# A mixture of experts behind an attention: the first layer's matmul with weights stationary and tokens moving

## The chip, the cores and the metric

The kernel runs on one core of one Trainium2 chip. The metric is the device time of one execution in microseconds (us), less being better. TensorE is called PE in the profile's rows (PEld is its weight load), VectorE DVE, ScalarE ACT, GpSimd POOL and SyncE SP.

## The reference

Two stages, in float32.

- **Attention.** q, k and v are 8 batches x 8 heads x 576 positions x 64. A coarse attention over positions averaged by four, and a local one within a band of three positions on either side, are added. The result is seen as 4608 tokens of 512 values.
- **Experts.** Each token goes to the one of eight experts whose embedding it is most alike (cosine, divided by a temperature); `gate_w` is the softmax weight of that expert. For the tokens of expert e:

```
h = np.maximum(x[mask] @ w1[e], 0.0)
out[mask] = gate_w[mask, None] * (h @ w2[e])
```

w1[e] is 512 x 1024, w2[e] is 1024 x 512.

## The kernel before

**Attention phase** (from the start to about 320 us of the trace). It goes over 32 units (a batch and a pair of heads) in a software pipeline, writes each batch's tokens with their expert scores to a scratch `xd` in HBM, and keeps each token's expert and its rank. The first expert's weights are prepared beside it.

**Expert phase** (from about 320 to 803 us). The tokens, sorted by expert, fill slots of 128 (`SLOT`); 41 slots run here, and five more stand behind a branch that is not taken. Each slot q goes through these steps:

- `gather` (POOL): an indirect DMA brings the slot's 128 token rows into `xg`.
- `x_size` and `x_split`: the tokens are scaled by a power of two and split into two fp16 halves (high and low), one on ACT, the other on DVE. A transposing DMA on SP's queue (line 1030) makes `xT`, with the 512 values on the partitions in four pieces and the tokens along the free dimension.
- `mm1` (line 1066): for each half n of the 1024 hidden values, 12 matmuls in `mm1_half` (lines 1076 to 1078) fill one PSUM bank [128 tokens, 512]. The stationary operand is a 128x128 piece of `xT`, and 512 columns of w1 move. There are three products for each of the four pieces k: x high with w1 high, x high with w1 low, x low with w1 high.
- `hidden`: ACT writes relu as fp16 (line 1085), DVE the remainder as fp16 (line 1086), both into `h2` [tokens, 2, 512], of which there are two buffers. A transposing DMA on SP's queue (line 1089) makes half of `hT`, with the hidden values on the partitions. It is two such DMAs a slot.
- `mm2_part`: 24 matmuls (lines 1101 to 1103) with a 128x128 piece of `hT` stationary and 512 columns of w2 moving. `out_rows` scales by the gate on ACT, and `store` writes the rows with an indirect DMA on POOL's queue.

`run_slots` writes the order out by hand. For slot q it is mm1(q), with hidden(q); the test for new weights; the next gather; x_size and x_split of slot q+2; then mm2(q-1), its output and store. So PE runs mm1(q), mm2(q-1), mm1(q+1), mm2(q), and hT(q) has from the end of mm1(q) to the end of mm1(q+1) to arrive.

**A change of expert** happens seven times. The weights (float32, staged in `st`) are split into fp16 high and low by `split_all`, in four pieces of 128x1024: `w1h` on ACT (line 773), `w1l` on DVE (line 774). Piece p of w1 holds two of the four k (by p % 2) and half the hidden values (by p // 2), so pieces 0 and 1 make up half n = 0. The split of w1 stands between mm1(q) and mm1(q+1), that of w2 behind mm2(q-1). After the split, SP loads the next expert's 2 MB into `st` (line 866); that load stands in SP's queue ahead of the transpose for xT(q+2). Where the flag says that no new weights are needed, these loads move nothing.

SP's queue, in program order for a slot: two transposes for hT, the loads of w1, the transpose for xT(q+2), the loads of w2. POOL's queue carries gathers and stores.

**The way into the phase** (`run`, lines 1140 to 1193): mm1(0) is interleaved with the end of the attention by calls of `mm1_half` with a range of k; then come mm1(1), the first three pieces of mm2(0), the lists of the first four slots (`ids_of`, line 594: PE, then DVE), x_split(2), the rest of mm2(0), mm1(2).

Of the kernel before, what the change touches and what calls it, by code (L numbers as in the profile page):

```python
# [9 lines left out]
F16 = mybir.dt.float16  # L10
BF16 = mybir.dt.bfloat16
I32 = mybir.dt.int32
AF = mybir.ActivationFunctionType
ALU = mybir.AluOpType
# [6 lines left out]
N, DM, E, FF = B * S, H * D, 8, 1024  # L21
# [9 lines left out]
SLOT = 128  # L31
# [17 lines left out]
class Kern:  # L49
# [1017 lines left out]
        for n in range(2):  # L1067
            self.hidden(q, n, self.mm1_half(q, n))

    def mm1_half(self, q, n, k0=0, k1=DM // 128, ps=None):  # L1070

        nc, xT = self.nc, self.sl[q]["xT"]
        ps = self.bank() if ps is None else ps
        ns = slice(n * 512, (n + 1) * 512)
        for k in range(k0, k1):
            nc.tensor.matmul(out=ps, lhsT=xT[:, 0, k], rhs=self.w1h[:, k, ns], start=(k == 0), stop=False)  # L1076
            nc.tensor.matmul(out=ps, lhsT=xT[:, 0, k], rhs=self.w1l[:, k, ns], start=False, stop=False)  # L1077
            nc.tensor.matmul(out=ps, lhsT=xT[:, 1, k], rhs=self.w1h[:, k, ns], start=False, stop=(k == self.KC - 1))  # L1078
        return ps

    def hidden(self, q, n, ps):

        nc, s = self.nc, self.sl[q]
        h2 = self.hd.tile([SLOT, 2, 512], F16, name="h2")
        nc.scalar.activation(out=h2[:, 0], in_=ps, func=AF.Relu)  # L1085
        nc.vector.scalar_tensor_tensor(out=h2[:, 1], in0=ps, scalar=0.0, in1=h2[:, 0], op0=ALU.max, op1=ALU.subtract)  # L1086
        if not n:
            s["hT"] = self.hd.tile([128, 2, 2, 4, SLOT], F16, name="hT")
        nc.sync.dma_start_transpose(out=s["hT"][:, n].rearrange("p t c s -> p (t c) s"),
                                    in_=h2.rearrange("p a f -> p (a f)"))  # L1090

    def mm2(self, q):
        self.out_rows(q, self.mm2_part(q))
# [1 line left out]
    def mm2_part(self, q, j0=0, j1=FF // 128, ps=None):  # L1095

        nc, s = self.nc, self.sl[q]
        ps = self.bank() if ps is None else ps
        for j in range(j0, j1):
            hh, hl = (s["hT"][:, j // 4, t, j % 4] for t in range(2))  # L1100
            nc.tensor.matmul(out=ps, lhsT=hh, rhs=self.w2h[:, j, :], start=(j == 0), stop=False)  # L1101
            nc.tensor.matmul(out=ps, lhsT=hh, rhs=self.w2l[:, j, :], start=False, stop=False)  # L1102
            nc.tensor.matmul(out=ps, lhsT=hl, rhs=self.w2h[:, j, :], start=False,  # L1103
                             stop=(j == self.FC - 1))
        return ps
# [134 lines left out]
```

## Time and profile before

| | |
|---|---|
| median of three runs | 820.86 us (820.54 to 826.13) |
| the profiled execution | 818.35 us, of it a span of 816.6 us from the first instruction to the last |
| PE busy, share of the span | 725.5 us, 89% |
| PE weight loads | 424.7 us, 52% |
| DVE, ACT, POOL busy | 520.1, 514.4, 400.9 us |
| mean granted TensorE clock | 0.950 |
| queue q1 (SP), share of 16 DMA engines | 64.5% |

Times in rows are in us from the span's start unless marked ns. "Idle before" is time in which the engine did nothing ahead of an instruction, with what ended it. A granted clock of 1.00 is TensorE at 2.4 GHz, 0.50 at 1.2 GHz. A matmul's recorded duration is that of one through its pipeline; they overlap, so the pace of a row of them is read from start to start.

### The profile page before, as it was taken

The page shows a single profiled execution, that of the slowest core. Times are in us where ns is not written, and L with a number is a line of the kernel's source. Part 1 is how long each engine was busy: PE and PEld are TensorE (multiplying, and loading weights), DVE is VectorE, ACT ScalarE, POOL GpSimd, SP SyncE. Part 2 cuts the span into 40 slices and gives each one's busy share as a digit, 9 for nine tenths or more (in the row PEclk, how much of TensorE's full clock was granted, in tenths as well). Part 3 has the DMA queues.
Part 4 walks back from the last instruction along what each step waited for, and adds up shares of the span by engine and source line. Part 5 has one row for each costly group of instructions (what it writes and reads, how often), then busy time and mean ns, then how long its engine had stood idle before and what let it go on. Part 6 is the DMA issues. An engine that isn't in the chain of part 4 may idle for free. (4 is left out here: it accounts for less than half of the span.)

```text
span 816.6 us, 22314 instructions
## 1 busy us (share of the span) xinstructions
PE 725.5 (89%) x7588; PEld 424.7 (52%) x7588; DVE 520.1 (64%) x1597; ACT 514.4 (63%) x1159; POOL 400.9 (49%) x783
## 2 busy tenths in 40 slices
PE   7799799988899989688989899989998998999993
PEld 4577677766677766343444444434443444444441
DVE  7698798998789898574735647364653355456420
ACT  6678788889779764236754767566664356547520
POOL 6364645475454563364544455564554435544421
PEclk9899898999889889899999999999999999999997
DMA  7578787877767736946887978889698659759750
GB/s 177 122 185 204 196 200 147 222 141 230 121 180 149 183 65 205 214 117 114 224 167 127 282 151 233 181 218 226 173 213 136 133 159 215 162 111 256 146 104 18
DMA packets 246901, 138.93 MB, mean 170 GB/s; under 512 B 177106, under 2 KB 223186, under 8 KB 246752
## 3 DMA queue, kind: packets, MB, share of 16 engines
q1 hardware_dynamic: 238944, 116.05, 64.5%
q0 software_dynamic: 6560, 19.03, 8.8%
q10 hardware_dynamic: 1248, 2.11, 1.0%
q8 instruction: 62, 1.02, 0.6%
q14 instruction: 87, 0.71, 0.3%
HBM read 213.05 MB, written 20.33 MB: 286 GB/s over the span
## 5 line engine op out<-in xcount | busy, mean ns | idle before, releaser
L1076 PE MATMUL bank<-w1h,xT 128*128 128x512 f16 x328 | 126.0, 384 | 16.2 <-DMA xT<-x 10.3
L1101 PE MATMUL bank<-w2h,hT 128*128 128x512 f16 x328 | 125.8, 383 | 15.1 <-DMA hT<-h 15.1
L1077 PE MATMUL bank<-w1l,xT 128*128 128x512 f16 x328 | 125.6, 383 | 1.3 <-DVEq L921 1.3
L1078 PE MATMUL bank<-w1h,xT 128*128 128x512 f16 x328 | 125.6, 383 | 0.0
L1102 PE MATMUL bank<-w2l,hT 128*128 128x512 f16 x328 | 125.6, 383 | 0.0
L1103 PE MATMUL bank<-w2h,hT 128*128 128x512 f16 x328 | 125.6, 383 | 0.0
L347 ACT ACTIVATE kq<-bank 64x288 f32<-64x288 f32 x256 | 109.7, 429 | 20.9 <-PE bank L343 16.2
L1086 DVE SCALAR_TENSOR_TENSOR h<-bank,h 128x512 f16<-128x512 f32 x82 | 55.2, 690 | 99.2 <-ACT h L1085 76.3
L1085 ACT ACTIVATE h<-bank 128x512 f16<-128x512 f32 x82 | 47.8, 594 | 103.9 <-PE bank L1078 53.9
L1114 POOL DMA_INDIRECT out_dram<-o,ids x41 | 45.7, 1116 | 133.9 <-ACTq L916 101.4
L361 POOL TENSOR_TENSOR pool_kq<-kq 128x288 f32<-128x288 f32 x62 | 41.6, 677 | 87.8 <-ACT kq L347 86.1
L998 POOL DMA_INDIRECT xg<-xd,ids x41 | 45.8, 1117 | 51.0 <-POOLq L922 15.5
L749 ACT ACTIVATE junk<-st 128x1024 bf16<-128x1024 f32 (+1 forms) x30 | 67.6, 2254 | 4.2 <-issue 2.8
L1076 PEld LDWEIGHTS <-xT 128*128 128x128 f16 x328 | 32.3, 99 | 55.5 <-DMA xT<-x 17.3
L1101 PEld LDWEIGHTS <-hT 128*128 128x128 f16 x328 | 34.7, 106 | 50.9 <-DMA hT<-h 16.2
L370 POOL TENSOR_TENSOR pool_v<-ld_v 72x256 f32<-72x256 f32 x64 | 47.0, 750 | 23.4 <-DMA ld_v<-in_v_dram 23.2
L1046 ACT ACTIVATE lg<-lg,lmx 128x8 f32<-128x8 f32 x41 | 12.3, 301 | 73.1 <-DVE lmx L1044 73.1
L67 POOL TENSOR_SCALAR nw_t<-nw_y,nw_a 128x1 f32<-128x1 f32 x120 | 52.4, 437 | 12.1
L409 ACT ACTIVATE ad<-bank,md 72x144 f32<-72x144 f32 x128 | 46.5, 370 | 18.6 <-DVE md L403 15.5
L1028 DVE SCALAR_TENSOR_TENSOR x<-xg,sc,x 128x512 f16<-128x512 f32 x41 | 30.9, 753 | 40.3 <-ACT x L1025 40.2
L1077 PEld LDWEIGHTS <-xT 128*128 128x128 f16 x328 | 32.4, 99 | 41.7 <-issue 5.7
L1078 PEld LDWEIGHTS <-xT 128*128 128x128 f16 x328 | 32.4, 99 | 41.2 <-issue 3.3
(220 smaller groups left out, 1592.1 us busy)
## 6 DMA issues: line engine op xcount, KB each, us to landing
st<-in_moe_w_dram SPq DMA_DIRECT2D x148, 1024.0 KB
ld_k<-in_k_dram SPq DMA_DIRECT2D x64, 144.0 KB
ld_q<-in_q_dram SPq DMA_DIRECT2D x64, 144.0 KB
ld_v<-in_v_dram SPq DMA_DIRECT2D x32, 288.0 KB
vw<-in_v_dram SPq DMA_DIRECT2D x64, 144.0 KB
xd<-xr SPq DMA_DIRECT2D x8, 1040.0 KB
st<-in_moe_w_dram SPq DMA_DIRECT2D x12, 512.0 KB
st<-in_moe_w_dram ACTq DMA_DIRECT2D x4, 512.0 KB
```

The costliest lines, as they stand in the source:

```text
L67: g.tensor_scalar(out=t, in0=y, scalar1=y, scalar2=a, op0=ALU.mult, op1=ALU.mult)
L347: nc.scalar.activation(out=kq[h * D:(h + 1) * D, w, 3 + r:3 + r + S:2], in_=ps[r * D:(r + 1) * D], func=AF.Copy)
L370: g.tensor_tensor(out=t6[:, c], in0=vr[:, :, 0:2 * D], in1=vr[:, :, 2 * D:], op=ALU.add)
L749: self.nc.scalar.activation(out=junk, in_=src, func=AF.Square, accum_out=acc)
L1076: nc.tensor.matmul(out=ps, lhsT=xT[:, 0, k], rhs=self.w1h[:, k, ns], start=(k == 0), stop=False)
L1077: nc.tensor.matmul(out=ps, lhsT=xT[:, 0, k], rhs=self.w1l[:, k, ns], start=False, stop=False)
L1078: nc.tensor.matmul(out=ps, lhsT=xT[:, 1, k], rhs=self.w1h[:, k, ns], start=False, stop=(k == self.KC - 1))
L1085: nc.scalar.activation(out=h2[:, 0], in_=ps, func=AF.Relu)
L1086: nc.vector.scalar_tensor_tensor(out=h2[:, 1], in0=ps, scalar=0.0, in1=h2[:, 0], op0=ALU.max, op1=ALU.subtract)
L1101: nc.tensor.matmul(out=ps, lhsT=hh, rhs=self.w2h[:, j, :], start=(j == 0), stop=False)
L1102: nc.tensor.matmul(out=ps, lhsT=hh, rhs=self.w2l[:, j, :], start=False, stop=False)
L1103: nc.tensor.matmul(out=ps, lhsT=hl, rhs=self.w2h[:, j, :], start=False, stop=(j == self.FC - 1))
```

## The change

In `mm1_half` the operands change places: a 128x128 piece of w1 is stationary and the slot's 128 tokens (128 columns of `xT`) move. For each half n there are four groups c of 128 hidden values, each with all four k in turn and the same three products, and each with its own quarter of the bank. The bank then holds [128 hidden values, 4 x 128 tokens], which is the layout that mm2 takes as its stationary operand. So ACT and DVE write straight into `hT`; `h2` and the transposing DMA of line 1089 are gone. A slot's first layer has 96 matmuls of 128 columns, each with its weight load, in place of 24 of 512 columns. The calls that split `mm1_half` in `run` keep their numbers, which now mean a range of c.

```diff
-    def mm1_half(self, q, n, k0=0, k1=DM // 128, ps=None):
+    def mm1_half(self, q, n, c0=0, c1=4, ps=None):
 
         nc, xT = self.nc, self.sl[q]["xT"]
         ps = self.bank() if ps is None else ps
-        ns = slice(n * 512, (n + 1) * 512)
-        for k in range(k0, k1):
-            nc.tensor.matmul(out=ps, lhsT=xT[:, 0, k], rhs=self.w1h[:, k, ns], start=(k == 0), stop=False)
-            nc.tensor.matmul(out=ps, lhsT=xT[:, 0, k], rhs=self.w1l[:, k, ns], start=False, stop=False)
-            nc.tensor.matmul(out=ps, lhsT=xT[:, 1, k], rhs=self.w1h[:, k, ns], start=False, stop=(k == self.KC - 1))
+        for c in range(c0, c1):
+            o, f = ps[:, c * SLOT:(c + 1) * SLOT], slice((4 * n + c) * 128, (4 * n + c + 1) * 128)
+            for k in range(self.KC):
+                nc.tensor.matmul(out=o, lhsT=self.w1h[:, k, f], rhs=xT[:, 0, k], start=(k == 0), stop=False)
+                nc.tensor.matmul(out=o, lhsT=self.w1h[:, k, f], rhs=xT[:, 1, k], start=False, stop=False)
+                nc.tensor.matmul(out=o, lhsT=self.w1l[:, k, f], rhs=xT[:, 0, k], start=False, stop=(k == self.KC - 1))
         return ps
 
     def hidden(self, q, n, ps):
 
         nc, s = self.nc, self.sl[q]
-        h2 = self.hd.tile([SLOT, 2, 512], F16, name="h2")
-        nc.scalar.activation(out=h2[:, 0], in_=ps, func=AF.Relu)
-        nc.vector.scalar_tensor_tensor(out=h2[:, 1], in0=ps, scalar=0.0, in1=h2[:, 0], op0=ALU.max, op1=ALU.subtract)
         if not n:
-            s["hT"] = self.hd.tile([128, 2, 2, 4, SLOT], F16, name="hT")
-        nc.sync.dma_start_transpose(out=s["hT"][:, n].rearrange("p t c s -> p (t c) s"),
-                                    in_=h2.rearrange("p a f -> p (a f)"))
+            s["hT"] = self.hd.tile([128, 2, 2, 4 * SLOT], F16, name="hT")
+        h = s["hT"][:, n]
+        nc.scalar.activation(out=h[:, 0], in_=ps, func=AF.Relu)
+        nc.vector.scalar_tensor_tensor(out=h[:, 1], in0=ps, scalar=0.0, in1=h[:, 0], op0=ALU.max, op1=ALU.subtract)
```

In `mm2_part` only the slice that names a piece of `hT` changes.

## Rows read from the trace of the kernel before

**Rows 1.** The profile page: busy time by engine, then the costliest groups of instructions on TensorE, with busy us, mean ns of one | idle us of the engine just before them and what ended it (one of the three matmul lines of either layer; the last row is a weight load, on PEld).

```profile
PE 725.5 (89%) x7588; PEld 424.7 (52%) x7588; DVE 520.1 (64%) x1597; ACT 514.4 (63%) x1159; POOL 400.9 (49%) x783
...
L1076 PE MATMUL bank<-w1h,xT 128*128 128x512 f16 x328 | 126.0, 384 | 16.2 <-DMA xT<-x 10.3
L1101 PE MATMUL bank<-w2h,hT 128*128 128x512 f16 x328 | 125.8, 383 | 15.1 <-DMA hT<-h 15.1
...
L1076 PEld LDWEIGHTS <-xT 128*128 128x128 f16 x328 | 32.3, 99 | 55.5 <-DMA xT<-x 17.3
```

**Rows 2.** Busy time of each engine in stretches of the run: us, then busy us (and instructions) of PE, PEld, DVE, ACT and POOL, the granted TensorE clock, the busy share of the DMA engines, GB/s. The first is in the attention phase, the others in the expert phase.

```profile
150.00:200.00 50.00, 44.12 (x952) 34.20 (x950) 46.06 (x136) 43.81 (x125) 28.60 (x39) 1.00 0.88 215
380.00:803.00 423.00, 397.38 (x1861) 182.71 (x1859) 213.55 (x648) 238.10 (x375) 203.59 (x473) 1.00 0.81 178
620.00:660.00 40.00, 40.00 (x193) 18.76 (x192) 14.82 (x58) 15.14 (x33) 18.04 (x45) 1.00 0.63 124
616.00:620.00 4.00, 3.51 (x10) 1.35 (x11) 1.98 (x7) 3.43 (x3) 0.84 (x3) 0.57 0.97 209
```

**Rows 3.** TensorE in order of time at 343 to 359 us: start us, us from the first start to the last end, what, and in brackets the idle time before it.

```profile
343.07 0.38 PE L1101 MATMUL bank<-w2h,hT 128*128 128x512 f16 x1
...
346.09 0.38 PE L1103 MATMUL bank<-w2h,hT 128*128 128x512 f16 x1
349.27 0.39 PE L1076 MATMUL bank<-w1h,xT 128*128 128x512 f16 x1 [2.80 <-DMA xT<-x]
...
353.34 0.38 PE L1078 MATMUL bank<-w1h,xT 128*128 128x512 f16 x1
...
355.93 0.38 PE L1078 MATMUL bank<-w1h,xT 128*128 128x512 f16 x1
356.14 1.64 PE L594 MATMUL bank<-parts,at 128*128 128x78 bf16 x40
357.62 0.38 PE L1101 MATMUL bank<-w2h,hT 128*128 128x512 f16 x1
```

**Rows 4.** TensorE's matmuls and its weight loads around 299 us, in order of time.

```profile
299.01 0.90 PE L594 MATMUL bank<-parts,at 128*128 128x6 bf16 x30
...
298.95 0.87 PEld L594 LDWEIGHTS <-at 128*128 128x128 bf16 x30
```

**Rows 5.** TensorE by groups of instructions from 380 to 803 us: busy us, mean ns | idle us before, and what ended it.

```profile
L1101 PE MATMUL bank<-w2h,hT 128*128 128x512 f16 x304 | 115.9, 381 | 9.3 <-DMA hT<-h 9.3
...
L1076 PE MATMUL bank<-w1h,xT 128*128 128x512 f16 x292 | 111.0, 380 | 11.9 <-DMA xT<-x 7.1 <-ACT w2h L773 2.3 <-ACT junk L749 1.7
```

**Rows 6.** Who waited for whom from 340 to 812 us: us in all, times, longest.

```profile
ACT h L1085 <- DMA hT<-h: 34.6, 13, 6.8
```

**Rows 7.** TensorE in order of time at 612 to 618 us.

```profile
616.49 0.61 PE L1101 MATMUL bank<-w2h,hT 128*128 128x512 f16 x1 [4.03 <-DMA hT<-h]
...
617.32 0.63 PE L1103 MATMUL bank<-w2h,hT 128*128 128x512 f16 x1
```

**Rows 8.** The SP queue in order of time around 604 us.

```profile
599.88 2.36 SPq L866 DMA_DIRECT2D st<-in_moe_w_dram  x2
603.52 6.06 SPq L1089 DMA_TRANSPOSE hT<-h  x2
...
610.62 5.21 SPq L1030 DMA_TRANSPOSE xT<-x  x1
```

**Rows 9.** The start of the expert phase, 327 to 345 us, in order of time on each engine: TensorE, VectorE, ScalarE, the SP queue.

```profile
331.99 0.38 PE L1078 MATMUL bank<-w1h,xT 128*128 128x512 f16 x1
338.15 0.61 PE L1101 MATMUL bank<-w2h,hT 128*128 128x512 f16 x1 [5.78 <-DMA hT<-h]
...
341.96 0.21 PE L594 MATMUL bank<-parts,at 128*128 128x8 bf16 x1
...
334.64 0.32 DVE L586 TENSOR_TENSOR parts<-eq,tlo 128x160 bf16<-128x160 f32 x1
...
343.73 0.75 DVE L1028 SCALAR_TENSOR_TENSOR x<-xg,sc,x 128x512 f16<-128x512 f32 x1
...
341.84 0.60 ACT L1085 ACTIVATE h<-bank 128x512 f16<-128x512 f32 x1 [3.04 <-DMA hT<-h]
...
327.78 16.64 SPq L1089 DMA_TRANSPOSE hT<-h  x4
344.52 1.28 SPq L1030 DMA_TRANSPOSE xT<-x  x1
```

**Rows 10.** A change of expert, 577 to 597 us, in order of time: the last matmul of a first layer, the split of the new first weights on VectorE, the next first layer, then SP's loads of the following expert's weights, SP's transpose of x, and the first layer after next.

```profile
577.34 0.38 PE L1078 MATMUL bank<-w1h,xT 128*128 128x512 f16 x1
...
581.43 2.49 DVE L774 SCALAR_TENSOR_TENSOR w1l<-st,wscl,w1h 128x1024 f16<-128x1024 f32 x2 [1.71 <-ACT w1h L773]
...
582.87 0.38 PE L1076 MATMUL bank<-w1h,xT 128*128 128x512 f16 x1
...
585.24 1.49 SPq L866 DMA_DIRECT2D st<-in_moe_w_dram  x2
...
589.28 1.23 SPq L1030 DMA_TRANSPOSE xT<-x  x1
...
596.49 0.39 PE L1076 MATMUL bank<-w1h,xT 128*128 128x512 f16 x1 [1.77 <-DMA xT<-x]
```

More of the change, by code (lines that the diff above doesn't have):

```diff
@@ L1099, in mm2_part @@
         for j in range(j0, j1):
-            hh, hl = (s["hT"][:, j // 4, t, j % 4] for t in range(2))
+            hh, hl = (s["hT"][:, j // 4, t, j % 4 * SLOT:(j % 4 + 1) * SLOT] for t in range(2))
             nc.tensor.matmul(out=ps, lhsT=hh, rhs=self.w2h[:, j, :], start=(j == 0), stop=False)
```

## The prediction

> **What bounds the kernel now.** I read the page's first and fifth parts first. PE is busy for 89% of the span, and its costliest groups are the six matmul lines of the two layers, about 126 us each; the idle time ahead of them is 16.2 us for xT and 15.1 us for hT [rows 1]. An average over two phases says little about a change in one, so I cut the run into stretches. From 380 to 803 us PE is busy for 397.4 of 423 us at a granted clock of 1.00, and in a calm stretch for all of 40 us, with the DMA engines at 0.63 [rows 2]. In that phase PE sets the pace. The reader is to see two stores of time there: the pace of the matmuls, and 25.6 us of waits. Of the waits, the groups of PE's instructions in that stretch name 9.3 us for hT, 7.1 for xT, 2.3 behind the split of w2 and 1.7 behind a long Square on ACT [rows 5].
>
> The change puts one store against the other: it ends the wait for hT and makes the first layer's matmuls shorter and four times as many.
>
> **The pace of the new matmuls.** The order of time on PE gives the pace of the old ones: 14 steps from 343.07 to 346.09 us, 215.7 ns for 512 columns [rows 3]. At 2.4 GHz 512 columns are 213.3 ns, so 2.4 ns are lost at each. The trace has no f16 matmul of 128 columns. The nearest row is line 594: 40 matmuls of 78 columns, each with its own 128x128 weight load in a 2-byte type, start at 356.14 us and the next line starts at 357.62 [rows 3]. That is 37.0 ns for a pair, 4.5 ns more than 78 columns (32.5 ns). With 6 columns, 30 such pairs take 0.90 us and their 30 loads 0.87 us, so a pair is under 30 ns even where nothing covers the load [rows 4]. In the 78-column row the load is therefore covered nearly whole by the columns: 29 + 32.5 would be 61.5 ns, not 37.0.
>
> For 128 columns (53.3 ns) this gives 53.3 + 2.4 to 53.3 + 4.5, 55.7 to 57.8 ns; I take the middle, 56.8. A slot's first layer is then 96 x 56.8 ns = 5.45 us against 24 x 215.7 ns = 5.18 us: +0.28 us, and +11.3 us over 41 slots. The bounds: 53.9 ns, a quarter of the old pace, costs nothing; 99 ns, the recorded duration of one weight load if nothing covered it [rows 1], makes 9.50 us a slot and +177 us. The 78-column row is far nearer to the first.
>
> **Where the growth is hidden.** At a change of expert the rows show what ends last. The first layer of the first slot with new weights starts at 582.87 us, and the next one at 596.49 waits 1.77 us for xT, whose transpose SP issues at 589.28 behind the 2 MB load issued at 585.24 [rows 10]. That chain hangs on the end of the first layer at 577.34, through the split, and not on PE's work in between. So growth there is swallowed by the wait. It also swallows a new one: before, the first half's k = 2 comes after 6 matmuls (1.29 us), now after 6 of 128 columns in its first group, and the w1 low that it needs is the ninth matmul, 0.45 us after the start, 583.32. The second piece of w1l is done at 583.92 [rows 10]: a wait of 0.60 us. Together 0.88 us, against 0.9 to 2.3 us of wait after such a slot: in [rows 5] four waits for xT (7.1 us), the 2.3 that follow the split of w2, and one of 0.9 among the rest make six of the seven changes. One change pays the 0.60. **Growth: 35 x 0.28 + 0.60 = +10.3 us.**
>
> **What goes.**
> - Waits for hT between 380 and 803 us: 9.3 us [rows 5]. The largest, 4.03 us at 616.49 [rows 7], arises since SP issues both transposes at 603.52 behind a 2 MB load of 599.88 and needs 6.06 us for it [rows 8]. Late next is xT for the slot after, issued at 610.62 and taking 5.21 us behind the same crowd [rows 8]; mm2 of 5.2 us from 612.5 lies over it, until 617.6. I take **-9.3**.
> - The granted clock was 0.57 from 616 to 620 us, after that wait [rows 2], which is mostly the lower level; the pace there is 0.43 us, from 616.49 to 617.32 in two steps [rows 7]. Some 3 us at half pace: **-1.5**.
> - ACT waited 34.6 us for buffers of h2 that transposes still read [rows 6]. The three waits of PE behind ACT's Square, 1.7 us [rows 5], follow that delay: **-1.7**.
> - The start. PE stops at 332.2 us and waits 5.78 us for hT(0); SP is held 16.64 us by four transposes, and ACT waits with hidden(1) until 341.84 [rows 9]. The transpose of xT(2) goes out at 344.52, after DVE's split at 343.73 [rows 9], and mm1(2) starts at 349.27 [rows 3]. Without hT, PE can pass the three pieces of mm2(0) by 335 and come to the lists, whose input DVE has ready at 334.96 [rows 9]. From the lists (341.96) to mm1(2) (349.27) it was 7.31 us; 335.0 + 7.31 = 342.3: **-7.0**, with the wait for xT(2) still in it.
>
> **What costs nothing.** ACT and DVE write the same 128x512 elements as before, into other memory. The buffer of hT that they write was read by mm2(q-2), which PE finished ahead of mm1(q): no wait. Nothing is queued behind the removed transposes on SP but the loads and xT, which can only come earlier. POOL's queue is not touched. Supply of instructions: a slot has 2 x (96 + 24) on PE, in some 11 us (423 us for 304 / 8 = 38 slots), 22 per us; the attention phase sustains 38 per us with the DMA engines at 0.88 [rows 2]. Were that cover gone, it would show as idle time "issue" ahead of the new lines.
>
> **Sum.** On the profiled execution's own 818.35 us: +10.3 - 9.3 - 1.5 - 1.7 - 7.0 = -9.2, 809.2 us. The median of the runs shown is 820.86, 2.5 us above that execution, so I state 809.2 + 2.5 = 812 us.
>
> **Rivals.**
> 1. *The load is not covered* (slower). Between matmuls of the same short length in hundreds of pairs, a load has to wait for the matmul ahead. Its place is lines of `mm1_half`, its price the load's own 29 ns [rows 4] on top of 53.3: 82 ns a pair, 7.90 us a slot, +112 us in place of the growth, 913 us. It decides early: at 58.9 ns a pair the gains are eaten, and above 61 ns the kernel is slower by 1%. Against it stands the 78-column row; for it, that this row is only 40 pairs long. The Trainium skill ("TensorE: Matmul & The Clock Gate", section "Back-to-back issue gap") gives about 81 ns for a matmul of 128 columns in a stream of loads and matmuls; by that figure a slot would grow by 2.6 us and the time be about 908. The same section gives 131 ns for 512 columns, where this trace has 215.7 [rows 3], so the measurement decides and I give the rule little. Chance 0.14, half of it between 61 ns and the full price.
> 2. *The wait changes its name.* xT is late where hT was, since the loads of weights, not the transposes, fill the queue [rows 8, 10]. Then 9.3 + 1.5 + 1.7 stay and only the start gains: 821.7 + 2.5 = 824 us. For it: the transpose of x needed 5.21 us in one such place. Against it: with hT gone the queue holds a third of the transposes. Chance 0.27, partial forms included.
> 3. *More is freed.* The waits for xT at changes (7.1 + 2.3 + 0.9 us) go too: 801 us. Against it: that chain has a split and a 2 MB load that the change leaves. Chance 0.11.
>
> The forecast has 0.48. That the change does nothing can be left out: the removed DMA is in the diff.
>
> **Numbers.** A measurement of this kernel can tell about 1% from no change: faster is below 812.7 us, slower above 829.1. The forecast lies on that border, and its bounds of pace alone move it by 4 us either way; I count 0.34 of its 0.48 as faster and 0.14 as within. Rival 3 is faster, rival 2 within but for 0.02, rival 1 slower. Faster 0.47, same 0.39, slower 0.14. The range runs from rival 3 to just above rival 2, 801 to 826; rival 1 and a little below are left out. The forecast's own range is 806 to 818.
>
> **What would show it.** The pace of 96 matmuls in a calm slot: 55.7 to 57.8 ns from start to start. No idle time for hT by DMA ahead of line 1101's successor; what stands there must be ACT or DVE, and short. mm1(2) at about 342 us. At changes, a wait for w1l inside the first half, and the wait for xT still there but shorter. A pace above 61 ns, or xT's idle time risen from 16.2 us [rows 1] to above 25, would make the prediction wrong.

## The result, and the profile after

The changed kernel took **798.6 us** (median of four runs, 793.9 to 801.5) beside 823.5 us for the kernel before: a ratio of 0.969 [0.963, 0.976]. The forecast was 812 us with a range of 801 to 826, so the sign was right and the time lay 2.4 us below the range. Two repeats, run beside the experiments, gave 805.1 us (0.978 [0.968, 0.987]) and 804.8 us (0.979 [0.976, 0.983]), inside the range and still below the forecast. So whether the time falls in or just under the range is scatter; that the gain is larger than forecast is not: it is 17 to 25 us (24.9, and 17.5 and 18.4 in the repeats) where 9.2 were worked out. Executions of one kernel fall in a fast and a slow state; ratios, with their 95% intervals, compare fast ones alone, while medians are of all.

The page of the profiled execution (797.77 us, span 796.0), with the lines that answer to [rows 1]:

```profile
PE 730.8 (92%) x10540; PEld 549.4 (69%) x10540; DVE 518.5 (65%) x1597; ACT 514.7 (65%) x1159; POOL 402.6 (51%) x783
...
q1 hardware_dynamic: 152352, 94.55, 47.6%
...
L1077 PE MATMUL bank<-xT,w1h 128*128 128x128 f16 x1312 | 225.5, 221 | 9.1 <-DMA xT<-x 7.7
...
L1100 PE MATMUL bank<-w2h,hT 128*128 128x512 f16 x328 | 124.2, 379 | 0.0
```

PE is busy 5 us longer in a span that is 20.6 us shorter. The wait for hT, 15.1 us before, is gone from the second layer (whose first line is 1100 now), the idle time ahead of the first layer has fallen from 16.2 to 9.1 (of it for xT 10.3 and 7.7), and queue q1 takes 47.6% of the DMA engines' time where it took 64.5%. (225.5 us for a line of 1312 matmuls is the sum of recorded durations of 221 ns, which overlap; it isn't the line's share of the run.)

The expert phase as one stretch, and then by groups of TensorE's instructions, as in [rows 2, 5]:

```profile
380.00:782.00 402.00, 396.17 (x4420) 286.67 (x4418) 210.76 (x642) 234.84 (x371) 199.36 (x461) 1.00 0.48 138
```

```profile
L1079 PE MATMUL bank<-xT,w1l 128*128 128x128 f16 x1152 | 195.2, 219 | 0.2
...
L1077 PE MATMUL bank<-xT,w1h 128*128 128x128 f16 x1152 | 195.2, 219 | 5.1 <-DMA xT<-x 4.8 <-ACT x L1025 0.3
...
L757 PE MATMUL bank<-wsq,onesf 128*128 128x2 f32 x70 | 12.1, 242 | 0.5
```

Of 402 us PE is idle for under 6, where it was 25.6 of 423. The DMA engines fell from 0.81 to 0.48.

TensorE in order of time through one slot's first layer, in a calm stretch (first matmul, last matmul, the next line):

```profile
624.66 0.22 PE L1077 MATMUL bank<-xT,w1h 128*128 128x128 f16 x1
...
629.96 0.22 PE L1079 MATMUL bank<-xT,w1l 128*128 128x128 f16 x1
630.02 0.22 PE L757 MATMUL bank<-wsq,onesf 128*128 128x2 f32 x1
```

95 steps in 5.30 us are **55.8 ns** from start to start. A first layer takes 5.36 us where it took 5.18.

The start of the phase, TensorE and then the SP queue, as in [rows 9]:

```profile
334.71 1.16 PE L594 MATMUL bank<-parts,at 128*128 128x8 bf16 x40 [0.48 <-DVE parts L586]
...
341.50 0.23 PE L1077 MATMUL bank<-xT,w1h 128*128 128x128 f16 x1 [2.38 <-DMA xT<-x]
...
337.17 1.25 SPq L1030 DMA_TRANSPOSE xT<-x  x1
```

The 5.78 us of wait for hT are now 0.48 for DVE, SP issues xT(2) at 337.17 instead of 344.52, and mm1(2) starts at 341.50 instead of 349.27.

A change of expert, the same one as in [rows 10]: the split of w1 low on VectorE, two weight loads of TensorE, and the first layer after next.

```profile
567.35 4.90 DVE L774 SCALAR_TENSOR_TENSOR w1l<-st,wscl,w1h 128x1024 f16<-128x1024 f32 x4 [1.39 <-ACT w1h L773]
...
569.90 0.10 PEld L1079 LDWEIGHTS <-w1l 128*128 128x128 f16 x1 [0.20 <-DVE w1l L774]
575.07 0.30 PEld L757 LDWEIGHTS bank<-wsq,onesf 128*128 128x128 f32 x2 [0.25 <-ACTq L916]
...
581.73 0.22 PE L1077 MATMUL bank<-xT,w1h 128*128 128x128 f16 x1 [1.07 <-DMA xT<-x]
```

The ninth matmul does wait for the second piece of w1l, but 0.20 us, not 0.60. The wait at line 757 for ACT, which the forecast didn't count (4.0 us over the seven changes before, 0.5 after), is 0.25 us here.

**Where the time went, by parts of the expert phase.** From the start of mm1(0) to the start of the second layer that follows the last first layer the profiled executions took 471.2 us before, and 451.0, 456.2 and 456.6 in the three profiles of the changed kernel. Summed from PE's order of time, as differences to before in us:

| part | forecast | after | repeat 1 | repeat 2 |
|---|---|---|---|---|
| mm1(0) to mm1(2) (28.37 before) | -7.0 | -7.4 | -7.4 | -7.5 |
| first layers from mm1(2) on (212.05 before) | +10.3 | +4.9 | +5.8 | +4.6 |
| between a first layer and the second layer behind it (18.83 before) | -9.3 | -8.6 | -8.4 | -8.4 |
| second layers with the waits behind them (211.92 before) | -3.2 | -9.1 | -5.0 | -3.3 |
| sum | -9.2 | -20.2 | -15.0 | -14.6 |

(The forecast's clock and ACT terms, 1.5 and 1.7, stand in the fourth line; its growth of mm1(0) and mm1(1), 0.6, in the second.) Two lines differ. The second does in every execution, by 4.5 to 5.7 us. The fourth does by 0.1 to 5.9, and differs as much between executions of one kernel.

### The profile page after: what moved, and what is told of

Same layout as the page of the kernel before. It is cut to its first block, busy times and chain, and to the rows that moved or that the text cites. A ratio compares the mean times of both kernels' runs of the same rounds, so it can differ in the third digit from the quotient of the medians.

```text
span 796.0 us, 27977 instructions
## 1 busy us (share of the span) xinstructions
PE 730.8 (92%) x10540; PEld 549.4 (69%) x10540; DVE 518.5 (65%) x1597; ACT 514.7 (65%) x1159; POOL 402.6 (51%) x783
## 3 DMA queue, kind: packets, MB, share of 16 engines
q1 hardware_dynamic: 152352, 94.55, 47.6%
## 5 line engine op out<-in xcount | busy, mean ns | idle before, releaser
L1077 PE MATMUL bank<-xT,w1h 128*128 128x128 f16 x1312 | 225.5, 221 | 9.1 <-DMA xT<-x 7.7
L1079 PE MATMUL bank<-xT,w1l 128*128 128x128 f16 x1312 | 225.5, 221 | 1.6 <-DVEq L921 1.4
L1078 PE MATMUL bank<-xT,w1h 128*128 128x128 f16 x1312 | 225.4, 221 | 0.0
L1077 PEld LDWEIGHTS <-w1h 128*128 128x128 f16 x1312 | 129.4, 99 | 16.6 <-ACTq L917 5.5
L1078 PEld LDWEIGHTS <-w1h 128*128 128x128 f16 x1312 | 129.5, 99 | 3.6
L1079 PEld LDWEIGHTS <-w1l 128*128 128x128 f16 x1312 | 129.5, 99 | 3.0 <-DVEq L921 1.6
L1102 PE MATMUL bank<-w2h,hT 128*128 128x512 f16 x328 | 124.3, 379 | 0.0
L1100 PE MATMUL bank<-w2h,hT 128*128 128x512 f16 x328 | 124.2, 379 | 0.0
L1089 DVE SCALAR_TENSOR_TENSOR hT<-bank,hT 128x512 f16<-128x512 f32 x82 | 55.2, 689 | 83.3 <-ACT hT L1088 52.2
L1088 ACT ACTIVATE hT<-bank 128x512 f16<-128x512 f32 x82 | 47.7, 594 | 83.1 <-PE bank L1079 68.6
L998 POOL DMA_INDIRECT xg<-xd,ids x41 | 45.6, 1112 | 43.5 <-issue 14.6
L67 POOL TENSOR_SCALAR nw_t<-nw_y,nw_a 128x1 f32<-128x1 f32 x120 | 53.3, 444 | 12.1
L1102 PEld LDWEIGHTS <-hT 128*128 128x128 f16 x328 | 32.0, 98 | 38.8
L1100 PEld LDWEIGHTS <-hT 128*128 128x128 f16 x328 | 35.0, 107 | 33.9
L409 ACT ACTIVATE ad<-bank,md 72x144 f32<-72x144 f32 x128 | 46.6, 371 | 17.4 <-DVE md L403 14.6
```

The source lines that it names most:

```text
L67: g.tensor_scalar(out=t, in0=y, scalar1=y, scalar2=a, op0=ALU.mult, op1=ALU.mult)
L1077: nc.tensor.matmul(out=o, lhsT=self.w1h[:, k, f], rhs=xT[:, 0, k], start=(k == 0), stop=False)
L1078: nc.tensor.matmul(out=o, lhsT=self.w1h[:, k, f], rhs=xT[:, 1, k], start=False, stop=False)
L1079: nc.tensor.matmul(out=o, lhsT=self.w1l[:, k, f], rhs=xT[:, 0, k], start=False, stop=(k == self.KC - 1))
L1088: nc.scalar.activation(out=h[:, 0], in_=ps, func=AF.Relu)
L1089: nc.vector.scalar_tensor_tensor(out=h[:, 1], in0=ps, scalar=0.0, in1=h[:, 0], op0=ALU.max, op1=ALU.subtract)
```

## The experiments

They ask four things: whether the removed transposes cost anything beyond the waits that name them, what the buffers of h2 were worth by themselves, what the remaining waits hang on, and what sets the pace of the short matmuls. The theories go by letters, told in each expectation.

**Repeat 1: the changed kernel again.**

> The changed kernel once more, beside the runs of the same call. Theory A (the gain is TensorE's waits for hT and what hangs on them; the rest of the DMA traffic is as it was): 794 to 802 us, with waits for xT at the changes of expert summing to 5 us in one profile and up to 10 in another, since they depend on how long the 2 MB load takes in that execution. Theory B (fewer transposes also make the other transfers land sooner): the same time, and the waits for xT at the changes again 5 us or less, the load again 6.4 us on average.

805.1 us, 0.978 [0.968, 0.987], beside 822.5 us for the kernel before. The waits for xT at changes of expert came to 6.8 us in place of 4.8, and after the longest of them (3.65 us) a first layer took 6.98 us. So a gain in this wait of a few us is within what executions of one kernel differ by.

**Idle transposes.** The changed kernel, with the transposes of before put back into a buffer that nobody reads (four buffers each of `hT` and `void`); nothing is left out.

```diff
+        void = self.hd.tile([128, 8, SLOT], F16, name="void", bufs=4)
+        nc.sync.dma_start_transpose(out=void, in_=h.rearrange("p t s -> p (t s)"))
```

> The changed kernel with the two transposes of a slot put back as traffic: each half of hT is transposed into a buffer that nothing reads, on the same queue at the same place, and with four buffers so that neither ScalarE nor TensorE waits for them. Theory A: 794 to 804 us, no more than 3 us above the changed kernel, waits for xT at the changes 5 to 10 us. Theory B: the start loses some 3 to 5 us again and the waits for xT and for the loads grow to 10 us and more: 806 to 814 us.

813.4 us, 0.987 [0.983, 0.991]: 8 us above the repeat beside it, with intervals that just overlap. The start: the SP queue, ScalarE's queue with the loads of the second weights, VectorE's split of x of slot 2, and TensorE's first layer behind it:

```profile
329.44 3.88 SPq L1091 DMA_TRANSPOSE void<-hT  x2
339.26 3.17 SPq L1091 DMA_TRANSPOSE void<-hT  x2
342.52 1.26 SPq L1030 DMA_TRANSPOSE xT<-x  x1
...
333.64 1.96 ACTq L866 DMA_DIRECT2D st<-in_moe_w_dram  x4
...
340.23 0.75 DVE L1028 SCALAR_TENSOR_TENSOR x<-xg,sc,x 128x512 f16<-128x512 f32 x1
...
347.66 0.29 PE L1077 MATMUL bank<-xT,w1h 128*128 128x128 f16 x1 [6.57 <-DMA xT<-x]
```

In the changed kernel, whose mm1(0) starts at 320.52 (here at 322.49), ScalarE's queue and VectorE's split stand so:

```profile
327.14 0.40 ACTq L866 DMA_DIRECT2D st<-in_moe_w_dram  x1
...
336.39 0.75 DVE L1028 SCALAR_TENSOR_TENSOR x<-xg,sc,x 128x512 f16<-128x512 f32 x1
```

xT(2) goes out 20.0 us after the start of mm1(0), and not 16.7, and PE waits 6.57 us for it instead of 2.38. Two things delay it. The split of x that it reads ends 18.5 us after that start, and not 16.6; then the third and fourth transpose still hold SP until 342.43. So of these 3.4 us 1.5 belong to the transposes in the queue. The other 1.9 come by ScalarE, which begins its loads of the second weights 11.2 us after the start of mm1(0), and not 6.6, and so comes later to the relu of mm1(1) and to x. The run with four buffers of h2 (below) shows such a delay too (9.5 us), the kernel before with its two does not (6.5 us): in these four runs it goes with the four buffers, not with the transposes; what ScalarE waits for was not followed.

From 380 us on the waits ahead of first layers came to 11.5 us in place of 7.7, but those for xT to 7.1 in place of 6.8, and the load takes 6.43 us on average as without the transposes; the rest of the difference stands behind ScalarE. So theory B had the time, but its mechanism shows only at the start. Of the 17.5 us by which repeat 1 is faster than before, about 9 come without removing the transposes. How many of the other 8 the transposes themselves cost stays open: the start loses 4.2 (mm1(0) to mm1(2): 25.2 us, 21.0 in repeat 1), of which the queue's 1.5 are shown.

**Four buffers of h2, in the kernel before.** The operands stay as they were.

```diff
-        h2 = self.hd.tile([SLOT, 2, 512], F16, name="h2")
+        h2 = self.hd.tile([SLOT, 2, 512], F16, name="h2", bufs=4)
```

> The kernel before with four buffers of h2 in place of two, and nothing else: ScalarE no longer waits for transposes that still read. Theory A: TensorE's waits for hT (15 us) stay, those behind ScalarE (1.7 us) go and the start gains 1 to 3 us: 2 to 5 us below the kernel before. Theory C (ScalarE, held up by the buffers, was what made hT and xT late): 10 us or more below it.

816.4 us, 0.993 [0.989, 0.998]: a third of the gain of repeat 1 for one argument, a little more than expected. TensorE at the start, then its group of line 1101 from 380 us on:

```profile
332.52 1.16 PE L594 MATMUL bank<-parts,at 128*128 128x8 bf16 x40 [0.70 <-DVE parts L586]
...
341.84 0.61 PE L1076 MATMUL bank<-w1h,xT 128*128 128x512 f16 x1 [4.91 <-DMA xT<-x]
```

```profile
L1101 PE MATMUL bank<-w2h,hT 128*128 128x512 f16 x296 | 114.1, 386 | 13.1 <-DMA hT<-h 13.1
```

The hT wait of the start goes (mm1(0) to mm1(2): 23.4 us, 28.4 before) and PE's waits behind ACT's Square too, but from 380 us on the waits for hT come to 13.1 us. Buffers cure what waits for a buffer; what waits for the transpose itself stays.

**Other pieces of w1.** The changed kernel, with each of the four pieces of the split holding all k of a quarter of the hidden values, so that the first groups c find their weights complete.

```diff
-        n, k = FF // 2, 2 * self.KC // NP
-        return t[:, p % 2 * k:(p % 2 + 1) * k, p // 2 * n:(p // 2 + 1) * n]
+        n = FF // NP
+        return t[:, :, p * n:(p + 1) * n]
```

> The changed kernel with the weights of the first layer split in pieces of all four k and a quarter of the hidden values, so that the first two groups c need the first piece alone. The wait for w1 low inside the first layer after a change (0.4 us, seven times) goes. Theory A (at a change the chain through the split, the load and the transpose of x sets the end, so the wait for xT grows by the same): 0 to 1 us below the changed kernel. Theory D (TensorE's own work sets the end there): 3 us below it.

826.5 us, 1.011 [1.006, 1.016]: 1% slower than the kernel before, which neither theory foresaw. A first layer behind a change, the granted clock under it (the second to last columns as in [rows 2]), and the group's waits from 380 us:

```profile
595.76 0.27 PE L1077 MATMUL bank<-xT,w1h 128*128 128x128 f16 x1 [6.70 <-DMA xT<-x]
```

```profile
595.76:603.90 8.14, 8.14 (x97) 8.14 (x97) 1.36 (x5) 0.60 (x1) 5.27 (x13) 0.64 0.88 315
```

```profile
L1077 PE MATMUL bank<-xT,w1h 128*128 128x128 f16 x1124 | 198.1, 224 | 25.7 <-DMA xT<-x 22.5 <-ACT w2h L773 3.2
```

The wait for w1l did go, and 0.27 us at line 757 took its place. What lost the time is the load: each half of `st` now feeds all four pieces, so the next expert's first weights begin to move 9.33 us after the start of the second layer ahead of the split, and not 8.14. It also lasts longer, 7.13 us on average in place of 6.43. SP still puts xT(q+2) behind that load; xT lands later, PE waits 25.7 us in place of 5.1 (7.7 and 9.3 in the repeats), and after waits as long as 6.7 us it runs the next first layer at a granted clock of 0.64 (8.1 us in place of 5.36).

**Repeat 2 and the transpose of x ahead of the load.** In `run_slots` the load of the next first weights moves behind x_split.

> The changed kernel, for the comparison in this call: 796 to 806 us. In the trace the waits for xT at the seven changes of expert sum to 5 to 8 us, and the 2 MB load of the first weights takes 6.4 us on average, as it does with the transposes there.

```diff
                 self.renew(0, b + 1)
-                self.stage_next(0, b + 1)
...
                 self.x_split(q + 2)
+            if q < last:
+                self.stage_next(0, b + 1)
```

> The changed kernel with the transpose of x issued ahead of the 2 MB load of the next first weights on SP's queue, and nothing else. Theory A (at a change the first layer after next waits for xT, and xT waits for that load in the same queue): the transpose goes out 11.2 us after the second layer's start as before and lands some 2.5 us later, not 5 to 6; the waits for xT at changes go (5 to 8 us, and the low clock after the longest), 790 to 797 us, 5 to 8 below the changed kernel of this call. Theory D (TensorE's own work or ScalarE sets the end there): the wait takes another name, within 2 us of the changed kernel.

797.7 us, 0.972 [0.969, 0.975], beside 804.8 us, 0.979 [0.976, 0.983], for the changed kernel itself, whose waits at the changes came to 9.3 us here, 6.0 of them for xT. The SP queue at the same change of expert, then TensorE's groups from 380 us:

```profile
573.50 1.25 SPq L1031 DMA_TRANSPOSE xT<-x  x1
575.05 2.13 SPq L866 DMA_DIRECT2D st<-in_moe_w_dram  x4
```

```profile
L1080 PE MATMUL bank<-xT,w1l 128*128 128x128 f16 x1152 | 195.2, 219 | 0.7 <-DVE w1l L774 0.6
L1078 PE MATMUL bank<-xT,w1h 128*128 128x128 f16 x1152 | 195.2, 219 | 1.5 <-ACT junk L749 1.4
```

No wait for xT is left at any change. SP issues the transpose at the same time as before (11.16 us after the start of the second layer ahead of the split), but it has landed by 13.8 to 14.9, where it was 15.6 to 17.5 in the changed kernel's first profile, and the first layer after next starts at 16.4 to 16.8, where it was 17.3 to 17.9 on average in that kernel's three profiles and 18.1 before. So the wait hung on the load ahead of the transpose, and not on transposes.

**The start too.** The kernel of the run above, with x_split(2) moved to just behind mm1(1) and the Squares of the second weights around it shifted.

```diff
         self.mm1(1)
+        self.x_split(2)
         ps = self.mm2_part(0, 0, 3)
...
-        self.x_split(2)
         self.norms(2, self.nc.vector)
```

> As the run with x ahead of the load, and at the start of the expert phase the split of x of slot 2 stands ahead of the lists, and the four Squares of the second layer's weights stand in the idle time of ScalarE before the first gates. Theory A: mm1(2) starts 1 to 2 us sooner after mm1(0), the waits of 1.1 and 1.4 us before and in mm1(4) go with the low clock that follows: 3 to 6 us below the run with x ahead of the load, 786 to 794 us. Theory D: the lists come later by the split and take it back, 0.

795.1 us, **0.969 [0.965, 0.973]**, the fastest kernel of these runs; its interval overlaps that of the run above, so the further 2.6 us, less than the 3 to 6 expected, are not certain. The granted clock stays at 1.00 from 320 to 780 us; in the run above it was 0.50 from 368 to 371 us. Of the start's time 1.8 us go (mm1(0) to mm1(2) 19.1 us, 21.0 above). The start in TensorE's order of time:

```profile
337.92 1.16 PE L594 MATMUL bank<-parts,at 128*128 128x8 bf16 x40 [0.46 <-DVE parts L586]
342.89 0.23 PE L1078 MATMUL bank<-xT,w1h 128*128 128x128 f16 x1 [0.56 <-DMA xT<-x]
```

The wait for xT(2) is 0.56 us in place of 2.4, but 1.5 us of wait for DVE appear ahead of the next lists: part of the gain changed its name.

**The pace alone.** Eight rows of 64 matmuls, each with its own weight load, are added behind the end of the changed kernel.

> The changed kernel with eight rows of 64 matmuls at its end that nothing reads, each with its own 128x128 f16 weight load, of 512, 256, 128, 96, 80, 78, 64 and 32 columns. Theory E (a fixed 2.4 ns on top of the columns at 2.4 GHz, the load covered whole): 215.7, 109.1, 55.7, 42.4, 35.7, 34.9, 29.1 ns, and under 30 ns with 32 columns. Theory F (the loss grows as the columns get fewer, as the middle of the prediction had it): 56.8 with 128, 41 to 45 with 96, 37.0 with 78, 31 to 33 with 64.

```profile
800.92 13.99 PE L1200 MATMUL bank<-w1h,w2h 128*128 128x512 f16 x64 [3.31 <-ACTq L983]
814.74 7.15 PE L1202 MATMUL bank<-w1h,w2h 128*128 128x256 f16 x64
821.73 3.74 PE L1204 MATMUL bank<-w1h,w2h 128*128 128x128 f16 x64
825.30 2.88 PE L1206 MATMUL bank<-w1h,w2h 128*128 128x96 f16 x64
828.02 2.46 PE L1208 MATMUL bank<-w1h,w2h 128*128 128x80 f16 x64
830.31 2.41 PE L1210 MATMUL bank<-w1h,w2h 128*128 128x78 f16 x64
832.55 2.03 PE L1212 MATMUL bank<-w1h,w2h 128*128 128x64 f16 x64
834.42 1.75 PE L1214 MATMUL bank<-w1h,w2h 128*128 128x32 f16 x64
```

From one row's start to the next, divided by 64: 215.9 ns for 512 columns, 109.2, 55.8, 42.5, 35.8, 35.0, and 29.2 for 64. All are the columns at 2.4 GHz and 2.4 to 2.6 ns more. The weight load is covered whole down to 64 columns; with 32 a matmul starts every 25.1 ns in this trace, and something else than its columns (13.3 ns) sets the pace. And 78 columns take 35.0 ns, not the 37.0 that the forecast leaned on.

**Why 37.0.** Rows of 64 matmuls again, behind the end of the changed kernel, which differ from each other in one thing at a time.

> The changed kernel with seven rows of 64 matmuls of 78 columns (the last of 128) and their loads behind its end; nothing of the reference is left out. It asks which property of the lists of line 594 made them 37.0 ns a pair, where a row of 78 fp16 columns took 35.0: row 1 fp16 on one place, 2 bf16 on one place, 3 bf16 with the moving operand stepping by 160 bytes, 4 by 156 bytes, 5 by 156 bytes and accumulating as the lists do, 6 accumulating on one place, 7 the same of 128 columns. Theory F, accumulation into the same columns of the bank costs about 2 ns a pair: rows 1 to 4 at 35.0, rows 5 and 6 at 37, row 7 at 57 to 58 (then the first layer, which also accumulates, should not show 55.8: it changes its columns each 12 matmuls only). Theory G, the step of the moving operand costs it: 4 and 5 at 37, 1, 2, 3, 6 at 35.0, row 7 at 55.8. Theory H, it is the change to and from the row of lists, a fixed amount of some 0.08 us spread over 40 pairs: all rows of 64 between 35.0 and 36.3, row 7 at 55.8.

```profile
791.52 3.40 PE L1201 MATMUL bank<-w2h 128*128 128x78 f16 x64 [3.48 <-ACTq L983]
794.71 3.03 PE L1203 MATMUL bank<-at 128*128 128x78 bf16 x64
797.58 2.41 PE L1205 MATMUL bank<-at 128*128 128x78 bf16 x64
799.82 2.52 PE L1207 MATMUL bank<-at 128*128 128x78 bf16 x64
802.18 2.52 PE L1209 MATMUL bank<-at 128*128 128x78 bf16 x64
804.54 2.40 PE L1211 MATMUL bank<-at 128*128 128x78 bf16 x64
806.78 3.74 PE L1213 MATMUL bank<-at 128*128 128x128 bf16 x64
810.35 1.89 PE L1215 MATMUL bank<-w2h 128*128 128x512 f16 x8
```

Rows 3 to 7 are at 35.0, 36.9, 36.9, 35.0 and 55.8 ns: a moving operand that steps by 156 bytes from matmul to matmul costs 1.9 ns a pair, a step of 160 bytes or none costs nothing, and accumulation costs nothing. Theory G holds, for 156 bytes; which other steps cost was not tried. Rows 1 and 2 (49.8 and 44.8 ns) tell nothing of this, since the granted clock fell under them (below).

## Why the prediction came out as it did

The sign and the two large terms, the wait for hT and the start, were right by their mechanism. Two steps failed. The growth of the first layers was put at +10.3 us and came to +4.6 to +5.8, since the pace and the slots after a change were priced too high. And the waits for xT at the changes were left in the sum whole, 10.2 us; 5.1 to 9.3 of them were measured.

- **The pace: the term that was mis-sized.** "For 128 columns (53.3 ns) this gives 53.3 + 2.4 to 53.3 + 4.5 ...; I take the middle, 56.8." It is 55.8, the lower end. The upper end came from the lists of line 594 [rows 3], and their extra 2 ns are a matter of their moving operand's step, as the last experiment shows; the first layer's operand steps by multiples of 256 bytes. 1.0 ns x 96 x 41 is 3.9 us. The loss of 2.4 ns that the same rows gave for 512 columns was the better neighbour: it belongs to the matmul, not to its length.
- **The slots after a change.** "One change pays the 0.60", and the growth of the six others is swallowed by the wait for xT. Neither was so: the seven slots took 40.6 us together, 41.4 before. The wait for w1l is 0.2 us, and ahead of the growth stood the wait for ACT at line 757, which the forecast had not read. In the trace of before, from 340 us on:

```profile
L757 PE MATMUL bank<-wsq,onesf 128*128 128x2 f32 x74 | 11.1, 219 | 4.0 <-ACTq L916 4.0
```

  It swallowed the growth at all seven. Together with the pace this makes the growth about +5 in place of +10.3, in each of the three profiles: the part of the miss that is common to all.
- **The waits for xT at changes.** The forecast kept them, because the chain of split, load and transpose is untouched. The chain is: the load begins about 8.2 us and the transpose is issued 11.17 us after the start of the second layer ahead of the split, in both kernels. But the waits on it were 10.2 us (xT, the split of w2 and others) before and 5.1, 7.7 and 9.3 in the three profiles after. The load lasted 6.99 us on average in the profile of before and 6.43 to 6.54 in five others, those with transposes (idle transposes, four buffers of h2) among them; and the kernel before with four buffers of h2, transposes and all, had 4.5 us of these waits. So much of this term is that of one execution, and a forecast from a single profile can't place it better than by some 5 us. Rival 3 (801) came nearest to the time, but its mechanism gave 5.1 of its 10.2 us in the first profile and less in the others.
- **What held.** hT: -9.3 forecast, and no wait for hT is left. The start: -7.0 forecast, -7.4 measured. ACT's buffers and the clock after 616 us: neither wait nor low clock is left there. (That the waits behind ACT's Square came from h2's buffers is not shown: 1.4 us of them stand in the run with x ahead of the load, which has neither h2 nor its transposes.) ACT and DVE are as busy as before (514.7 and 518.5 us).
- **A reading that was wrong.** SP is not "held 16.64 us by four transposes" [rows 9]. That row merges four with a wait between them; the same queue in two windows:

```profile
327.78 5.89 SPq L1089 DMA_TRANSPOSE hT<-h  x2
339.56 4.87 SPq L1089 DMA_TRANSPOSE hT<-h  x2
```

  From 333.67 to 339.56 SP waits for the third one's input, which ACT's wait for a buffer of h2 makes late. The forecast of the start didn't use the 16.64. The other reading, "16.2 us for xT" [rows 1], is the whole idle time ahead of that line; xT is 10.3 of it.
- **Rival 1** (the load is not covered, 913 us) fell: 55.8 ns, with no idle time ahead of the new lines but the waits named above. The Trainium skill ("TensorE: Matmul & The Clock Gate", section "Back-to-back issue gap") gives 81 ns for such a stream of 128 columns and 131 for 512; these runs show 55.8 and 215.9. The formula that the same section of the Trainium skill keeps for a single matmul, the columns at 2.4 GHz and 2.5 ns, is what the streams here follow.
- **Rival 2** (the wait changes its name, 824) fell too: the wait for xT did not take the place of that for hT, in any of the three profiles. Its mechanism shows at the start of the run with idle transposes, where xT(2) goes out 1.5 us later behind them.

The three profiled executions are 20.6, 10.7 and 11.8 us shorter than that of before; the table's sums give 20.2, 15.0 and 14.6 of it. The rest lies almost whole in the attention phase, which the change leaves: its end (the start of mm1(0)) came 0.4 us sooner and 4.4 and 3.0 later than before, and between 315 and 328 us over all profiles, in no order of kernels. How the medians' 17 to 25 us divide was not followed beyond this.

## What to carry to other kernels

Price a short matmul by the loss that the long ones show at each instruction, and before a row of other matmuls is taken as its neighbour, look at what else differs in that row, such as the step of its operand. Before a merged row of a queue is read as time for which it is held, look at its parts: here over a third of 16.6 us was waiting for input. When traffic is put back to price it, check what else the extra buffers moved: here they came with a later start of ScalarE's loads, and the price of the traffic stays open. Before saying that a wait "swallows" growth, list all waits of that slot, small ones at a helper's line too, and move whatever is wanted next ahead of the big load in the queue; that was worth 7 us more here.

## Unexpected in the hardware

- A step of 156 bytes between the moving operands of successive matmuls cost 1.9 ns each (36.9 against 35.0 ns, one run).
- Behind an idle time of 3.48 us, PE ran rows of 78 columns without a gap, and the granted clock fell under them; the first stretch is ahead of that, the columns are those of [rows 2]:

```profile
791.50:792.50 1.00, 0.98 (x28) 0.99 (x29) 0.00 (x0) 0.00 (x0) 0.00 (x0) 1.00 0.03 8
...
793.50:794.60 1.10, 1.10 (x21) 1.10 (x19) 0.00 (x0) 0.00 (x0) 0.00 (x0) 0.50 0.05 15
...
796.70:797.50 0.80, 0.80 (x28) 0.80 (x26) 0.00 (x0) 0.00 (x0) 0.00 (x0) 1.00 0.00 0
```

  It went to the lower level (0.50, 1.2 GHz) while PE was busy and was back at 1.00 by 796.7. In the run with the row of 512 columns in that place, behind an idle time of 3.31 us, it stayed at 1.00. Why the one fell and the other did not stays open.
- A transpose for which SP has nothing ahead takes it 1.23 to 1.26 us; behind other transfers one took 5.21 us [rows 8].
